# A retention and mixture-of-experts kernel: operand preparation cut into steps, loads moved, second-weight sums from GpSimd to VectorE, last block stored in halves

## Chip, cores and metric

One core of a Trainium2 chip runs the whole kernel. The metric is the device time of one execution in microseconds: the median of several runs. The profile is one more execution, recorded by the hardware profiler. The engines are TensorE (PE in the profile; its weight loads are PEld), VectorE (DVE), ScalarE (ACT), GpSimd (POOL) and SyncE (SP), which here only issues transfers.

## The reference

The kernel computes retention (attention with a decaying state, batch 4, 8 heads, 768 positions, head size 64) and feeds its output to a mixture of 8 experts whose gate is normalised by 8 Sinkhorn rounds.

```python
for t in range(S):                      # retention
    state = gamma * state + outer(k[:, :, t], v[:, :, t])
    y[:, :, t] = scale * q[:, :, t] @ state
x = y as (3072, 512)

P = exp(x @ w_gate - max)               # gate
for _ in range(8):
    P /= P.sum(1, keepdims=True) + 1e-09
    P /= P.sum(0, keepdims=True) + 1e-09
    P *= N / E
for e in range(8):                      # experts
    h = maximum(x @ w1[e], 0.0)         # (3072,512) @ (512,1024)
    out += P[:, e:e + 1] * (h @ w2[e])  # (3072,1024) @ (1024,512)
```

## The kernel before

**Numbers in two parts.** Every operand of a large product is held as a rounded high part (fp32r) and a low remainder: `hi_act` (line 77) rounds on ScalarE, `lo` (line 80) subtracts the high part from the full value, on VectorE or GpSimd. A product is then three matmuls: high*high, low*high, high*low.

**Seven products for eight.** Both expert layers use a Strassen-like scheme: the 2x2 block products are made with seven products, called M1 to M7, on sums and differences of blocks. The operands of M1, M2, M3 and M7 (for x) or M1, M2, M4 and M7 (for w1) are loaded; the other three are made by four additions or subtractions.

**Opening stage: attention by blocks.** There are 24 blocks of 128 positions (6 chunks of 4 batches). Step `tau` of a loop written out by hand does, in this order: scale the keys of block tau (`decay_k`, L348, GpSimd), issue loads of block tau+3, split q and k of block tau+2 (`split_qk`: ScalarE rounds kh and QH, GpSimd makes kl, VectorE makes QL), scores of block tau+1 (L367 on PE, mask `ta` L370 on VectorE), gate logits of block tau-1, output of block tau (`attend`, L395 and L400 on PE, `RX` L404 on VectorE, stored to DRAM as `xd`), state update (`hold`, L379 on PE). Engines run their instructions in program order, and SP too. After steps 2 to 10 the remaining 13 blocks ride along in the rows of the next stage (`chunk(g, m)`), one block a row.

**First layer: 96 rows.** A unit (`UnitA`) is 256 columns of w1 (a job) on one third of x. A row n runs seven products in the order of `ROW`: (unit n: M6), (unit n+1: M1), (n: M3), (n: M7), (n+1: M2), (n+1: M5), (n: M4); m = 0 to 6 is the place in a row. Four PSUM banks are shared: the next product on a bank waits until VectorE (L213, L218, L225) or ScalarE (L207, L209, L211, L219, L226, L229) has read the one before. `sums` and `last_sum` make the sums that the second layer needs; all seven results are stored in DRAM as `hd`. In a row with attention, `chunk` adds one part at each m: m = 0 `decay_k` and `attend`, 1 logits, 2 scores, 3 `split_qk`, 4 `hold`, 5 loads.

**Preparing operands.** `w1_load(n)` brings job n's block into one of two halves of RW; `w1_tasks` makes its operand WA: four additions on GpSimd (L158) and two roundings on ScalarE in one task, then two remainders on VectorE as two tasks. A row takes one task at m = 0, 1 and 5. `x_load` brings a third of x from `xd` in eight transfers; `x_tasks` makes its operand in 22 tasks (two halves k of 4 subtractions and 7 roundings with remainder), shared between VectorE and GpSimd by a list. x of the first third (X0) is prepared in steps 9 and 10, that of the second (X1) from row 15 on VectorE alone, that of the third (X0 again) from row 33. Sinkhorn's 23 pieces (`sink`) come one after each of rows 26 to 47, the last after row 60.

**Second layer: 24 units of 28 parts.** `UnitB` is one expert on one third of x (experts in reverse). A part is a quarter (q) of a product: six matmuls. `b_part(s)` runs part s, evaluates a finished product (`post`, `emit`: L627, L629, L631 on VectorE, stored from SP for the first expert and by an accumulating GpSimd transfer, L636, for the others), issues loads of later h parts and converts part s+5 (`h_conv`: ScalarE rounds, VectorE makes the remainder). Beside it the next expert's w2 is prepared in two blocks f = 0, 1: `w2_load`, four subtractions on GpSimd (L719), then three roundings and three remainders; these tasks stand in a queue `bq`, one taken at q = 0, 2 and 3 of each product.

Of the kernel before, what the change touches and what calls it, by code (L numbers as in the profile page):

```python
# [28 lines left out]
NJ = E * QE  # L29
# [18 lines left out]
def kernel(  # L48
# [60 lines left out]
    def x_load(t, r):  # L109
        for i, c, d in ((M1, 0, 0), (M7, 1, 0), (M3, 1, 1), (M2, 0, 1)):  # L110
            for k in range(2):
                sp.dma_start(rd(t[:, XP[i], 1, k * 512:(k + 1) * 512]).rearrange("p (b s) -> p b s", s=C),
                             xd[2 * r + c][:, :, 2 * d + k, :])

    def x_tasks(t, engs):
        q = []
        sc = {M7: 0, M5: 1, M6: 2, M4: 3}
        e = [engs[k % len(engs)] for k in range(22)]
        for k in range(2):
            def w(i, a=1, k=k):  # L120
                return t[:, XP[i], a, k * 512:(k + 1) * 512]

            def src(i, w=w):
                return XSC[:, sc[i], :] if i in sc else rd(w(i))

            def tt(o, a, b, src=src):
                eng = e.pop()
                q.append(lambda: eng.tensor_tensor(XSC[:, sc[o], :], a, b, ALU.subtract))

            def one(i, w=w, src=src):  # L130
                eng = e.pop()

                def f():
                    hi_act(w(i, 0), src(i))
                    lo(eng, w(i, 1), src(i), w(i, 0))
                q.append(f)

            b12 = rd(w(M7))
            tt(M5, b12, src(M1))
            tt(M6, src(M3), src(M5))  # L140
            tt(M7, src(M3), b12)
            tt(M4, src(M2), src(M6))
            for i in (M1, M5, M2, M6, M7, M3, M4):
                one(i)
        return q
# [8 lines left out]
    def w1_tasks(n, eng_add, eng_lo):  # L154
        a, x = WA[n % 3], w1_raw(n)

        def tt(o, p, q, op):
            eng_add.tensor_tensor(x[:, WP[o]], x[:, WP[p]], x[:, WP[q]], op)  # L158

        def adds():  # L160
            tt(M5, M7, M4, ALU.add)
            tt(M6, M5, M1, ALU.subtract)
            tt(M3, M2, M6, ALU.subtract)
            tt(M7, M1, M7, ALU.subtract)
            hi_act(a[:, 0:3, 0, :], x[:, 0:3, :])
            hi_act(a[:, 3:7, 0, :], x[:, 3:7, :])

        def rest(s):
            lo(eng_lo, a[:, s, 1, :], x[:, s, :], a[:, s, 0, :])

        return [adds, lambda: rest(slice(0, 3)), lambda: rest(slice(3, 7))]
# [85 lines left out]
    with tc.manual_schedule():  # L257
# [6 lines left out]
        if True:  # L264
# [184 lines left out]
            for tau in range(2, LAST):  # L449
                if tau == 2:  # L450
                    loads(4)
# [4 lines left out]
                if tau < LAST - 2:  # L456
                    loads(tau + 3)
                else:
                    loads(tau + 3, (1, 3) if tau == LAST - 2 else (1,))
                if tau < LAST - 1:  # L460
                    split_qk(tau + 2)
                scores(tau + 1)
                logits(tau - 1)
                attend(tau)
                for t in late.get(tau, [tau]):
                    hold(t)
                if tau >= LAST - 2:
                    loads(tau + 3, (0, 2))
                if tau == 4:
                    w1_load(0)  # L470
                    w1_load(1)
                    todo += w1_tasks(0, pool, dve) + w1_tasks(1, pool, dve)
                if tau == 2 * B - 1:
                    x_load(X0, 0)
                if tau == 2 * B:
                    todo += x_tasks(X0, [dve, pool, dve])
                if tau in (6, 7):
                    run(todo, 3)
                if tau > 2 * B:
                    run(todo, 8)  # L480
# [119 lines left out]
        class UnitB:  # L600
# [37 lines left out]
            def post(self, i):  # L638
# [19 lines left out]
                elif i == M7:  # L658
                    self.emit(1, 1, ps, s5)
                elif i == M4:  # L660
                    self.emit(1, 0, ps, None)
# [55 lines left out]
        def w2_tasks(e, f):  # L717
            def tt(o, a, b):
                return lambda: pool.tensor_tensor(w2x[:, VP[o]], w2x[:, VP[a]], w2x[:, VP[b]], ALU.subtract)  # L719
# [9 lines left out]
            def two(a, b):  # L729
                return [lambda: hi(a, b), lambda: rest(a, b)]  # L730

            q, t, none = [tt(*x) for x in w2t], two(0, 3), [lambda: None]
            return ([lambda: w2_load(e, f)] + none * 6 + q[:2] + t[:1] + q[2:3] + t[1:] + q[3:] + none * 2
                    + two(3, 5) + two(5, 7))

        bq = []
# [3 lines left out]
        def b_part(s):  # L740
# [11 lines left out]
            e, g = divmod(u.n, NPAIR)  # L752
            if q != 1:
                run(bq, 1)
            if g == 0 and i == M6 and q == 0 and e + 1 < E:
                bq.extend(w2_tasks(e + 1, 0) + w2_tasks(e + 1, 1))
# [4 lines left out]
        w1_load(2)  # L761
# [4 lines left out]
        loaded = 3  # L766
        PS2 = None
        carry = None
        for n, u in enumerate(UA):
# [15 lines left out]
            if n == NJ + 1:  # L785
                xq = x_tasks(X0, [dve, pool])
# [9 lines left out]
            for m, (k, i) in enumerate(ROW):  # L796
# [8 lines left out]
                if m in (0, 1, 5):  # L805
# [3 lines left out]
                if m in (1, 6) or n >= NJ:  # L809
# [14 lines left out]
            if 26 <= n < 25 + len(sink):  # L824
                sink[n - 26]()
            if n == 60:
# [4 lines left out]
        for s in range(6, 9):  # L831
            h_conv(s)
        for s in range(4, len(parts)):
# [52 lines left out]
```

## Time and profile before

| | |
|---|---|
| median of 3 runs | 2089.88 us (2088.89 to 2090.1) |
| the profiled execution | 2088.59 us; span 2086.8 us |
| busy: PE, PEld | 1995.7 us, 1644.4 us |
| busy: VectorE, ScalarE, GpSimd | 1581.3, 1043.7, 532.3 us |
| transfers | 505.19 MB, mean 242 GB/s |

A row of a timeline gives start, duration, engine, line, operation, out<-in, shape and count; brackets hold the idle time of the engine before it and what ended it. A row of the view of waits gives the waiting instruction, what it waited for, the total in us, the number of times and the longest. A window row gives the stretch, its length, the busy time of each engine with its number of instructions, the granted share of the TensorE clock, the share of the transfer engines and GB/s. A row of the chain gives start, duration and what it was. Several equal instructions in succession are merged.

### The profile page before, as it was taken

The numbers are of one execution on the slowest core, as the hardware profiler recorded it, in microseconds if no ns is written. First come the engines' busy times: TensorE is split into PE (matmuls) and PEld (weight loads), VectorE is DVE, ScalarE is ACT, GpSimd is POOL, SyncE is SP. The second block draws the span as 40 slices with busy tenths as digits, with TensorE's granted clock in tenths as the row PEclk, the third lists the DMA queues.
The fourth block names the chain that finished last, engine by engine and source line by source line (L and its number), as shares of the span: only waits on it lengthen the run. The fifth ranks groups of instructions, "written<-read, shape, count | busy, mean of one in ns | idle before, by whom it ended". The sixth has DMA issues, their size and how long they took to land.

```text
span 2086.8 us, 28805 instructions
## 1 busy us (share of the span) xinstructions
PE 1995.7 (96%) x9273; PEld 1644.4 (79%) x9273; DVE 1581.3 (76%) x2024; ACT 1043.7 (50%) x1674; POOL 532.3 (26%) x498
## 2 busy tenths in 40 slices
PE   7689999999899999999999999999999999999997
PEld 7578887887688888888886887887878787787886
DVE  6778878987787666666667787878788787968765
ACT  3334445654444444444445555555555555555553
POOL 4655633341421221221132101112021111202001
PEclk9789999999999999999999999999999999999999
DMA  7547668777476666666667989999999999999996
GB/s 257 163 135 244 216 225 276 250 246 247 160 234 212 227 219 218 215 232 217 220 236 262 305 269 269 269 278 268 260 285 255 277 271 274 263 288 258 263 264 157
DMA packets 253337, 505.19 MB, mean 242 GB/s; under 512 B 27840, under 2 KB 40448, under 8 KB 251136
## 3 DMA queue, kind: packets, MB, share of 16 engines
q1 hardware_dynamic: 241088, 459.30, 66.0%
q0 software_dynamic: 12096, 44.05, 11.5%
q8 instruction: 72, 1.18, 0.2%
q14 instruction: 81, 0.66, 0.1%
HBM read 270.36 MB, written 232.88 MB: 241 GB/s over the span
## 4 chain that ended last, share of the span: by engine, by line
PE 72%; DVE 9%; DMA 7%; issue 5%; POOL 1%; ACT 1%; SPq 0%; DVEq 0%; POOLq 0%; ACTq 0%
PE psA L190 38%; PE psA L618 19%; PE psB L618 13%; DMA WA<-hd 5%; DVE WA L80 4%; POOL RW L158 1%; DMA rn<-kn 1%; DVE QL L80 1%; DVE X L80 1%; DMA hd<-OT 1%; DVE XSC L629 1%; PE psa L367 0%; DMA RW<-w 0%; DVE OT L240 0%; DVE OT L234 0%
## 5 line engine op out<-in xcount | busy, mean ns | idle before, releaser
L190 PE MATMUL psA<-X,WA 128*128 128x512 f32 x4032 | 942.8, 394 | 18.2 <-DVE OT L213 8.1
L190 PEld LDWEIGHTS psA<-X,WA 128*128 128x128 f32 x4032 | 757.1, 189 | 183.6 <-ACT OT L229 12.3
L618 PE MATMUL psA<-WA,X 128*128 128x512 f32 x2296 | 539.0, 391 | 18.9 <-DVE WA L80 18.7
L77 ACT ACTIVATE WA<-WA 128x512 fp32r<-128x512 f32 x668 | 402.9, 629 | 270.3 <-PE psB L618 117.5
L618 PEld LDWEIGHTS psA<-WA,X 128*128 128x128 f32 x2296 | 428.6, 188 | 118.5 <-DVE WA L80 29.3
L80 DVE TENSOR_TENSOR WA<-WA,WA 128x512 fp32r<-128x512 f32 x487 | 363.7, 791 | 108.4 <-ACT WA L77 99.6
L618 PE MATMUL psB<-WA,X 128*128 128x512 f32 x1728 | 406.0, 391 | 7.3 <-ACT WA L77 3.9
L158 POOL TENSOR_TENSOR RW<-RW 128x256 f32<-128x256 f32 x256 | 243.0, 959 | 573.7 <-DMA RW<-w 348.3
L618 PEld LDWEIGHTS psB<-WA,X 128*128 128x128 f32 x1728 | 323.7, 188 | 79.6 <-DVE WA L80 8.0
L219 ACT ACTIVATE OT<-OT 128x512 f32<-128x512 f32 x96 | 60.7, 632 | 267.6 <-DVE OT L218 267.6
L80 DVE TENSOR_TENSOR WA<-RW,WA 128x768 fp32r<-128x768 f32 (+1 forms) x128 | 155.8, 1217 | 49.0 <-ACT WA L77 47.2
L80 DVE TENSOR_TENSOR WA<-WA 128x512 fp32r<-128x512 f32 x181 | 139.5, 798 | 38.2 <-ACT WA L77 34.0
L636 POOL DMA_DIRECT2D out<-XSC x57 | 49.6, 870 | 465.0 <-DVE XSC L631 248.2
L213 DVE TENSOR_TENSOR OT<-psA,OT 128x512 f32<-128x512 f32 x96 | 66.1, 689 | 99.2 <-PE psA L190 99.1
L77 ACT ACTIVATE WA<-RW 128x768 fp32r<-128x768 f32 (+1 forms) x128 | 115.1, 947 | 34.9 <-POOL RW L158 24.9
L719 POOL TENSOR_TENSOR RW<-RW 128x512 f32<-128x512 f32 x56 | 86.5, 1582 | 89.1 <-DMA RW<-w 57.4
L226 ACT ACTIVATE OT<-OT 128x512 f32<-128x512 f32 x96 | 60.7, 632 | 93.6 <-DVE OT L225 93.6
L225 DVE TENSOR_TENSOR OT<-psA,OT 128x512 f32<-128x512 f32 x96 | 66.2, 690 | 51.3 <-ACT OT L219 45.3
L236 DVE TENSOR_TENSOR OT<-OT 128x512 f32<-128x512 f32 x96 | 91.6, 954 | 3.3
L646 ACT ACTIVATE OT<-psA 128x512 f32<-128x512 f32 x96 | 57.4, 598 | 72.0 <-PE psA L618 68.0
L229 ACT ACTIVATE OT<-psA 128x512 f32<-128x512 f32 x96 | 57.4, 597 | 69.6 <-PE psA L190 40.8
L240 DVE TENSOR_TENSOR OT<-OT 128x512 f32<-128x512 f32 x96 | 75.3, 785 | 20.6 <-ACT OT L229 17.5
(166 smaller groups left out, 1517.1 us busy)
## 6 DMA issues: line engine op xcount, KB each, us to landing
hd<-OT SPq DMA_DIRECT2D x672, 256.0 KB, 2.8
WA<-hd SPq DMA_DIRECT2D x668, 256.0 KB, 6.0
RW<-w SPq DMA_DIRECT2D x64, 512.0 KB, 4.5
out<-XSC POOLq DMA_DIRECT2D x57, 512.0 KB, 8.2
RW<-w SPq DMA_DIRECT2D x16, 1024.0 KB, 8.4
out<-OT POOLq DMA_DIRECT2D x27, 512.0 KB, 8.1
OT<-pd SPq DMA_DIRECT2D x23, 512.0 KB, 7.4
xd<-RX SPq DMA_DIRECT2D x24, 256.0 KB, 5.1
```

The source lines that it names most:

```text
L77: act.activation(o, i, AF.Copy)
L80: eng.tensor_tensor(o, full, rd(h), ALU.subtract)
L158: eng_add.tensor_tensor(x[:, WP[o]], x[:, WP[p]], x[:, WP[q]], op)
L190: pe.matmul(ps, w[:, a, k * P:(k + 1) * P], x[:, b, k * 512:(k + 1) * 512], start=i in PRE and k == 0 and m == 0, stop=k == 1 and m == 2, ...
L213: dve.tensor_tensor(c12, ps, u2, ALU.add)
L219: act.activation(o, o, AF.Relu)
L225: dve.tensor_tensor(o, ps, s1, ALU.add)
L226: act.activation(o, o, AF.Relu)
L236: dve.tensor_tensor(t["S2"], t["S1"], t["A11"], ALU.subtract)
L240: dve.tensor_tensor(self.new("S4"), self.t["A12"], self.t["S2"], ALU.subtract)
L618: pe.matmul(ps[d] if isinstance(ps, tuple) else ps[:, d, :], w[:, a, q * 256 + d * P:q * 256 + d * P + P], h[b], start=i in PRE and q == 0 ...
L719: return lambda: pool.tensor_tensor(w2x[:, VP[o]], w2x[:, VP[a]], w2x[:, VP[b]], ALU.subtract)
```

## The change

- `x_load` can load one of its two source chunks alone. For the first third of x, chunk 0 is issued after step 5 and chunk 1 after step 8, instead of both after step 7.
- `x_tasks` becomes 11 steps for each half: step n does one subtraction (n < 4, always VectorE) or one remainder, and, for n < 7, the rounding that a later step (three to five on) needs. Of the remainders GpSimd has two in seven where the list is `[dve, dve, pool]`. In steps 9 and 10 of attention two of them stand in each of five places instead of eight at the end.
- `w1_tasks` has four tasks: additions, rounding, remainder, remainder. Jobs 0 and 1 are spread over steps 5 to 8. `w1_load(2)` moves from the start of the rows to step 7, `w1_load(3)` from the end of row 0 to step 8. In rows the tasks stand at m = 0, 3, 5 and 6; at m = 3 the task is ahead of `chunk(g, 3)`, that is of `split_qk`.
- x tasks of the third third run at all m but 2.
- Sinkhorn's pieces start after row 39, the last after row 62.
- w2's subtractions run on VectorE, one at each q of M1; rounding and remainders stand in M5 and the first quarter of M4, block f = 0 in the expert's first row of products, f = 1 in the second. `w2_load` of block 1 is issued in M4 of the first row, that of the next expert's block 0 in the third row; for expert 1 ahead of the second layer's loop.
- The last output block is not accumulated by GpSimd: its old value is loaded, VectorE adds it, and SP stores it in two halves.

```diff
-    def x_load(t, r):
-        for i, c, d in ((M1, 0, 0), (M7, 1, 0), (M3, 1, 1), (M2, 0, 1)):
-            for k in range(2):
+    def x_load(t, r, which=(0, 1)):
+        for i, c, d in ((M1, 0, 0), (M2, 0, 1), (M7, 1, 0), (M3, 1, 1)):
+            for k in range(2) if c in which else ():
...
+            def step(n, w=w, src=src):
+                b12 = rd(w(M7))
+                hi = [M1, M2, M5, M6, M7, M3, M4][n] if n < 7 else None
+                if n < 4:
+                    o, a, b = [(M5, b12, src(M1)), (M6, src(M3), src(M5)), (M7, src(M3), b12), (M4, src(M2), src(M6))][n]
+                    dve.tensor_tensor(XSC[:, sc[o], :], a, b, ALU.subtract)
+                else:
+                    i = [M1, M5, M2, M6, M7, M3, M4][n - 4]
+                    lo(engs[n % len(engs)], w(i, 1), src(i), w(i, 0))
+                if hi is not None:
+                    hi_act(w(hi, 0), src(hi))
+
+            q += [lambda n=n, step=step: step(n) for n in range(11)]
...
+        def rounded():
             hi_act(a[:, 0:3, 0, :], x[:, 0:3, :])
             hi_act(a[:, 3:7, 0, :], x[:, 3:7, :])
...
-        return [adds, lambda: rest(slice(0, 3)), lambda: rest(slice(3, 7))]
+        return [adds, rounded, lambda: rest(slice(0, 3)), lambda: rest(slice(3, 7))]
...
+                some = (lambda: run(todo, 2)) if tau > 2 * B else lambda: None
...
-                    todo += w1_tasks(0, pool, dve) + w1_tasks(1, pool, dve)
-                if tau == 2 * B - 1:
-                    x_load(X0, 0)
-                if tau == 2 * B:
-                    todo += x_tasks(X0, [dve, pool, dve])
-                if tau in (6, 7):
-                    run(todo, 3)
-                if tau > 2 * B:
-                    run(todo, 8)
+                    wt = w1_tasks(0, pool, dve), w1_tasks(1, pool, dve)
+                if 5 <= tau <= 8:
+                    k = tau - 5
+                    for f in (wt[0][:1], wt[0][1:2] + wt[1][:1], wt[0][2:] + wt[1][1:2], wt[1][2:])[k]:
+                        f()
+                if tau == 5:
+                    x_load(X0, 0, (0,))
+                if tau == 7:
+                    w1_load(2)
+                if tau == 8:
+                    w1_load(3)
+                    x_load(X0, 0, (1,))
+                    todo += x_tasks(X0, [dve, dve, pool])
...
+                elif i == M4 and self.n < len(UB) - 1:
+                    self.emit(1, 0, ps, None)
                 elif i == M4:
-                    self.emit(1, 0, ps, None)
+                    o = out[2 * self.r + 1, 0].rearrange("p (d t) -> p d t", d=2)
+                    sp.dma_start(TB[0], o)
+                    for d in range(2):
+                        y, t = YS[0][:, d], [t for x, t in ps if x.start <= d < x.stop][0]
+                        dve.tensor_tensor(y, t[:, d % t.shape[1]], PB[1 + self.n % 2][:, 1, :], ALU.mult)
+                        dve.tensor_tensor(y, y, TB[0][:, d], ALU.add)
+                        sp.dma_start(o[:, d], y)
...
-                return lambda: pool.tensor_tensor(w2x[:, VP[o]], w2x[:, VP[a]], w2x[:, VP[b]], ALU.subtract)
+                return lambda: dve.tensor_tensor(w2x[:, VP[o]], w2x[:, VP[a]], w2x[:, VP[b]], ALU.subtract)
...
+            return {(f, M1, x): [t[x]] for x in range(4)} | {
+                (f, M5, 0): [h[0], r[0]], (f, M5, 1): [h[1]], (f, M5, 2): [r[1]], (f, M5, 3): [h[2]],
+                (f, M4, 0): [r[2]]}
...
+                if (g, i, q) == (0, M4, 1):
+                    w2_load(e + 1, 1)
+                if (g, i, q) == (2, M6, 0) and e + 2 < E:
+                    w2_load(e + 2, 0)
...
-                xq = x_tasks(X0, [dve, pool])
+                xq = x_tasks(X0, [dve, dve, pool])
...
-                if m in (0, 1, 5):
+                if m in (0, 3, 5, 6):
                     run(wq, 1)
                 if n < NROW:
                     chunk(LAST + n, m)
-                if m in (1, 6) or n >= NJ:
+                if m in (1, 6) or n >= NJ and m != 2:
                     run(xq, 1)
...
-            if 26 <= n < 25 + len(sink):
-                sink[n - 26]()
-            if n == 60:
+            if 39 <= n < 38 + len(sink):
+                sink[n - 39]()
+            if n == 62:
                 sink[-1]()
...
+        w2_load(1, 0)
         for s in range(4, len(parts)):
             b_part(s)
```

More of the change, by code (lines that the diff above doesn't have):

```diff
@@ L117, in x_tasks @@
         sc = {M7: 0, M5: 1, M6: 2, M4: 3}
-        e = [engs[k % len(engs)] for k in range(22)]
         for k in range(2):
@@ L124, in src @@
                 return XSC[:, sc[i], :] if i in sc else rd(w(i))
[L126 to L144, printed above, removed]
+            def step(n, w=w, src=src):
[10 more added lines that the diff above has]
+            q += [lambda n=n, step=step: step(n) for n in range(11)]
         return q
@@ L459 @@
                     loads(tau + 3, (1, 3) if tau == LAST - 2 else (1,))
+                some()
                 if tau < LAST - 1:
                     split_qk(tau + 2)
+                some()
                 scores(tau + 1)
+                some()
                 logits(tau - 1)
                 attend(tau)
+                some()
                 for t in late.get(tau, [tau]):
                     hold(t)
+                some()
                 if tau >= LAST - 2:
@@ L727, in rest @@
                 lo(dve, t[:, :, 1], w2x[:, a:b], t[:, :, 0])
[L729 to L736, printed above, removed]
+            t = [tt(*x) for x in w2t]
+            h = [lambda a=a, b=b: hi(a, b) for a, b in ((0, 3), (3, 5), (5, 7))]
+            r = [lambda a=a, b=b: rest(a, b) for a, b in ((0, 3), (3, 5), (5, 7))]
+            return {(f, M1, x): [t[x]] for x in range(4)} | {
+                (f, M5, 0): [h[0], r[0]], (f, M5, 1): [h[1]], (f, M5, 2): [r[1]], (f, M5, 3): [h[2]],
+                (f, M4, 0): [r[2]]}
+        w2p = {}
         nload = [NHL + 4]
@@ L751, in b_part @@
                 h_conv(s + 5)
[L752 to L756, printed above, removed]
+            e, g = divmod(u.n - (i in PRE), NPAIR)
+            if u.n >= (i in PRE) and e + 1 < E:
+                if (g, i, q) == (0, M6, 0):
+                    w2p.clear()
+                    w2p.update(w2_tasks(e + 1, 0) | w2_tasks(e + 1, 1))
+                for f in w2p.get((g, i, q), ()):
+                    f()
+                if (g, i, q) == (0, M4, 1):
+                    w2_load(e + 1, 1)
+                if (g, i, q) == (2, M6, 0) and e + 2 < E:
+                    w2_load(e + 2, 0)
         wq, xq = [], []
         NROW = NCHUNK - LAST + 1
-        w1_load(2)
         loaded = conv = 2
@@ L765 @@
             UA[0].post(i)
-        loaded = 3
+        loaded = 4
         PS2 = None
```

## The prediction

> **What bounds the kernel now.** First the page's busy table, slices and chain.
>
> ```profile
> PE 1995.7 (96%) x9273; PEld 1644.4 (79%) x9273; DVE 1581.3 (76%) x2024; ACT 1043.7 (50%) x1674; POOL 532.3 (26%) x498
> PE   7689999999899999999999999999999999999997
> PE 72%; DVE 9%; DMA 7%; issue 5%; POOL 1%; ACT 1%; SPq 0%; DVEq 0%; POOLq 0%; ACTq 0%
> ```
>
> TensorE (PE) is busy nearly everywhere and makes 72% of the chain, so the change can only win its idle places: the first three slices and small stalls later. The view of waits, for PE, names these:
>
> ```profile
> PE psA L618 <- DVE WA L80: 18.7, 22, 1.5
> PE psA L190 <- DVE OT L213: 8.1, 3, 4.2
> PE psa L395 <- DVE ta L370: 6.4, 1, 6.4
> PE psa L379 <- POOL rn L348: 6.3, 1, 6.3
> PE psA L190 <- ACT OT L229: 6.3, 11, 1.2
> ```
>
> PE waits for conversions in the second stage (L618), twice in the rows where the third x is prepared (L213), once each in attention and in row 1 (L395, L379), and a little in each of the rows that carry attention (L229). I price these five places and the end of the program.
>
> **1. Attention up to row 0 (40 to 112 us): loads and x preparation moved.**
>
> ```profile
> 65.62 6.21 SPq L112 DMA_DIRECT2D X<-xd  x8
> 78.17 0.63 ACT L77 ACTIVATE WA<-OT 128x512 fp32r<-128x512 f32 x1 [9.20 <-DMA OT<-kT]
> 40.00:112.00 72.00, 50.47 (x339) 44.42 (x338) 55.05 (x65) 22.61 (x37) 45.45 (x35) 0.79 0.50 164
> 102.25 0.69 DVE L128 TENSOR_TENSOR XSC<-X,XSC 128x512 f32<-128x512 f32 x1
> X<-xd SPq DMA_DIRECT2D x24, 256.0 KB, 5.4
> ```
>
> In the window rows the third to seventh numbers are busy PE, PEld, DVE, ACT and POOL. Eight x transfers hold SP's queue for 6.21 us ahead of block 11's k; ACT waits 9.20 us for it, VectorE behind ACT, and PE 6.4 us behind VectorE's ta (the third row of waits). The change issues four at step 5 (half, 3.1 us) ahead of block 9's loads, which have a whole step to land, and four at step 8. The wait comes back elsewhere: at step 7 SP waits with w1_load(2) until VectorE has finished job 0's remainders (behind it: block 11's loads), at step 8 with w1_load(3) for job 1's, and the second half of x follows. VectorE's first x step at step 9 reads M7 of that half, so VectorE stands about 5.4 us for it, with block 11's split queued behind. I keep 6.5 us of wait there. VectorE is idle 72.0 - 55.05 = 17 us of this stretch now; of the other 10.5 us I let three stay, as the steps no longer wait for ACT's rounding and POOL's part is smaller. VectorE takes 18 of the 22 x operations instead of 15: 3 x 0.69 = 2.1 us. Sum -10.5 + 3 + 2.1 = -5.4, say **-6** (ACT no longer waits for POOL's sums before its split); bounds -10 (idle time gone) and +3 (the second half lands one more 5.4 us late, less what filling saves). w1's sums on POOL one step earlier stand before decay_k(6), whose products PE has before a split it waits for anyway: 0, and 1.5 us if that split came sooner. x steps of rows 15 to 25 stay on VectorE with rounding one step ahead of them: 0, since PE has no wait for X there to lose.
>
> **2. Row 1's missing weights.**
>
> ```profile
> 130.72 1.42 SPq L152 DMA_DIRECT2D RW<-w  x2
> 138.29 3.60 POOL L158 TENSOR_TENSOR RW<-RW 128x256 f32<-128x256 f32 x4 [14.17 <-DMA RW<-w]
> 127.02 1.05 PE L395 MATMUL psa<-rq,st 128*128 128x128 f32 x8
> 151.34 1.05 PE L395 MATMUL psa<-rq,st 128*128 128x128 f32 x8
> ```
>
> Job 3's block is issued only at 130.72; POOL waits 14.17 us with decay_k queued behind, and PE 6.3 us for decay_k (L348 in the view of waits). From row 1's attention to row 2's it takes 24.3 us; a steady row, below, 15.5. The change loads job 3 in step 8, so **-8.8**. Bounds -9.4 (if the row then runs at PE's own 15.0: 15.5 less PE's 0.5 of waiting, below) and, if job 4 is late in its place, -2. SP's loads of later jobs wait for the remainder in product 6 instead of 5, 1.4 us later; they are issued two rows ahead of their use, so 0.
>
> **3. Rounding moved to product 3 of a row: a cost.** The steady row with attention:
>
> ```profile
> 242.78 0.69 DVE L225 TENSOR_TENSOR OT<-psA,OT 128x512 f32<-128x512 f32 x1
> 246.26 1.79 ACT L77 ACTIVATE WA<-RW 128x768 fp32r<-128x768 f32 x2
> 254.07 0.63 ACT L219 ACTIVATE OT<-OT 128x512 f32<-128x512 f32 x1 [5.53 <-DVE OT L218]
> 255.77 2.51 DVE L80 TENSOR_TENSOR QL<-rq,QH 64x512 fp32r<-64x512 f32 x2 [1.74 <-ACT QH L77]
> 258.31 0.69 DVE L225 TENSOR_TENSOR OT<-psA,OT 128x512 f32<-128x512 f32 x1
> 261.47 0.73 PE L190 MATMUL psA<-X,WA 128*128 128x512 f32 x2 [0.49 <-ACT OT L229]
> ```
>
> L225 to L225 is 15.53 us: VectorE works from L225 to L218 (M7's sum with s5, which L219 waits for), waits 1.74 us while ACT does L219 and the split's rounding, does QL, and reaches L225; from there ACT's L229 frees the bank PE waits for. ACT's 1.79 us of weight rounding now stands in ACT's idle 5.53 us. `rounded` at m == 3 is emitted after L219 and before split_qk, so ACT runs it inside VectorE's wait: 1.74 + 1.79 = 3.53 us, a row of 17.3. Rows 0 to 10 have a split: 11 x 1.79 = **+19.7**. Bounds: 0 if a cover exists that I don't see, and +25 with the clock: PE's gap grows from 0.5 to about 2.3 us.
>
> ```profile
> 50.40:53.80 3.40, 1.31 (x9) 0.92 (x8) 2.07 (x2) 2.62 (x4) 2.57 (x2) 1.00 1.00 372
> 53.80:57.20 3.40, 2.66 (x13) 2.66 (x13) 3.32 (x7) 0.00 (x0) 3.24 (x5) 0.51 0.09 30
> ```
>
> After 3.4 us with 1.31 us of PE work the granted clock (third number from the end) was 0.51. A gap of 2.3 us leaves 1.1 us of work in such a stretch, if the stretch holds it whole. Half clock for 3.4 us costs PE 1.7 us, in half of 11 rows +9; VectorE's chain sets the row and hides part of it, so I take +5.5. The Trainium skill (TensorE: Matmul & The Clock Gate, section Why this matters for your kernels) asks only that no gap exceed about 3 us; by that rule the +5.5 is excluded and the sum stays as below, while the row with two gaps of a us each, at half clock after it, shows that shorter ones can do it.
>
> **4. Rows 32 to 36 (third x) and Sinkhorn.**
>
> ```profile
> 527.29 1.06 ACT L77 ACTIVATE WA<-RW 128x1024 fp32r<-128x1024 f32 x1 [4.38 <-POOL RW L158]
> 531.12 11.81 PE L190 MATMUL psA<-X,WA 128*128 128x512 f32 x42 [4.15 <-DVE OT L213]
> 500.00:560.00 60.00, 50.88 (x204) 40.04 (x203) 48.44 (x68) 27.50 (x48) 29.92 (x23) 0.91 0.64 201
> 600.00:900.00 300.00, 299.11 (x1324) 247.24 (x1323) 200.31 (x285) 139.75 (x223) 55.93 (x65) 1.00 0.65 221
> ```
>
> ACT stands 4.38 us behind POOL's w1 sums; the x operands and then VectorE's L213 stand behind ACT; PE loses 8.1 us idle (L213 in the view of waits) and, at a mean clock of 0.91, 0.09 x 60 = 5.4. Three products between sums and rounding cover POOL's 4 us, and Sinkhorn is gone from these rows. VectorE is still fuller than a row (five x operations of 0.69 on some 7 us), so 3 us stay: **-10.5**, bounds -13.5 and -4. Sinkhorn in rows 39 to 62 costs 0: VectorE is busy 200 of 300 us there; were it full, PE would lose in those rows what it saves in these. P is then ready two rows later, some thirty before its first use.
>
> **5. The second stage: sums from POOL to VectorE.**
>
> ```profile
> 1290.20 4.36 DVE L80 TENSOR_TENSOR WA<-WA,WA 128x512 fp32r<-128x512 f32 x2
> 1291.18 2.81 POOL L719 TENSOR_TENSOR RW<-RW 128x512 f32<-128x512 f32 x2
> 1355.89 10.88 PE psA L618 x48
> 1409.07 4.38 DVE WA L80 x2
> 1528.05 4.38 DVE WA L80 x2
> 1350.00:1388.00 38.00, 38.00 (x169) 31.45 (x169) 26.40 (x38) 19.85 (x33) 3.45 (x4) 1.00 0.94 267
> RW<-w SPq DMA_DIRECT2D x16, 1024.0 KB, 8.4
> ```
>
> Two conversions take 4.36 us instead of 1.3 while POOL sums (2.81): VectorE gets almost nowhere beside POOL, and PE then waits (18.7 us in 22 places, the first row of waits). An expert takes 1528.05 - 1409.07 = 118.98 us; its 504 products at 10.88 for 48 need 114.24: 4.74 us lost, in six experts 28.4. On VectorE four sums are 4 x 0.69 = 2.8 us a row, remainders 1.74 + 2 x 1.22 = 4.2: with the clean row's 26.4 it is 33.4 of 38.1 us, no overload. The second block is issued in M4 and lands 8.4 us later, about 1 us after VectorE wants it, with conversions queued behind; these run five parts (6.8 us) ahead, so 0.6 us an expert stays: **-25**; bounds -28 and 0. Issuing the first block before expert 0 puts 4 us of transfer ahead of its h loads: **+1**, bounds 0 and +4.
>
> **6. The last block.**
>
> ```profile
> 2075.47 1.37 DVE L627 TENSOR_TENSOR XSC<-psA,OT 128x512 f32<-128x512 f32 x2 [3.29 <-PE psA L618]
> 2077.14 0.86 POOL L636 DMA_DIRECT2D out<-XSC  x1 [3.80 <-DVE XSC L627]
> out<-XSC POOLq DMA_DIRECT2D x57, 512.0 KB, 8.2
> hd<-OT SPq DMA_DIRECT2D x672, 256.0 KB, 2.8
> ```
>
> Now the store starts at 2077.14 and lands 8.2 us later. Then VectorE does 4 x 0.69 from 2075.47 and SP stores at 2078.2, landing 2.8 later at 2081.0 instead of 2085.3: **-4.3**. The load of the old block waits for nothing recent; YS[0]'s earlier store lands about when it is needed. Bounds -5 and -1.
>
> **Sum.** -6 - 8.8 + 19.7 - 10.5 - 25 + 1 - 4.3 = -33.9 us on the profiled execution's 2088.59: 2054.7. The three runs' median is 1.3 above it: **2056 us**.
>
> **Rivals.** *Rounding is hidden* (rows keep 15.5 us): 2056 - 20 = 2036; ACT's 5.53 us of idle time speaks for it, but ACT runs in order, against it. *Start and clock bad*: part 1 at +3 and half clock in rows, 2056 + 9 + 5.5 = 2070. *The sums only change engines*, and VectorE still loses PE its 4.7 us: 2056 + 25 = 2081; 33.4 of 38.1 us speaks against it. *On the other side*: the second block lands so late that VectorE stands on its first sum with all conversions behind it. To end slower than now by 4 us, the experts would have to lose 28.4 + 13 = 41 us, 6.9 each, beyond a lead of some 4.8 us (6.8 less about 2 for a conversion itself); the block would have to land about 20 us after its issue, against 8.4: over 2094. PE's 72% of the chain and a transfer share of 0.94 leave that unlikely, not excluded.
>
> **How the numbers follow.** Forecast 0.60 (its own range 2046 to 2066), hidden rounding 0.10, bad start 0.14, sums only moved 0.08, between 2086 and 2094 0.03, other side 0.05. Range 2037 to 2074 leaves some two in ten out. Changes within 0.2% (4 us) can't be told from none: faster 0.91, same 0.04, slower 0.05.
>
> **What would show it.** Step 3: L225 to L225 at 17.3 us, VectorE's wait before QL at 3.5. Step 2: no wait of L379 for L348. Step 4: no wait above 2 us for L213. Step 5: no POOL sums, experts 114.5 to 115 apart. Step 6: some 6 us from PE's end to the last landing. Experts still at 119, or PE waiting for conversions after the sums, would make it wrong; so would rows at 15.5.

## The result: the change is slower, 2102.9 us

| | median | range | ratio to before, 95% interval |
|---|---|---|---|
| before | 2089.88 us | 2086.03 to 2091.91 | |
| after | 2102.91 us | 2100.74 to 2112.02 | 1.0074, 1.0059 to 1.0089 |

The forecast was 2056 us. The profiled execution of after took 2102.91 us with a span of 2101.1 (before 2086.8), so the two traces differ by 14.3 us and can be compared directly.

The page after: busy engines, two rows of slices, the chain.

```profile
PE 2016.9 (96%) x9273; PEld 1669.0 (79%) x9273; DVE 1558.5 (74%) x2092; ACT 1037.9 (49%) x1674; POOL 443.9 (21%) x431
PE   8688898999999999999999999999999999999998
PEclk9788889999999999999999999999999999999999
PE 85%; DVE 7%; issue 3%; ACT 2%; DMA 2%; SPq 0%; POOL 0%; DVEq 0%; ACTq 0%
```

The same 9273 matmuls are busy 21 us longer. That points at the clock, and in the slices of 52.5 us the granted clock is low in the second (the opening, as before) and, which is new, in the third to sixth, 105 to 315 us: the rows with attention. The view of waits for PE says the same. Line numbers shift: L221, L225, L186 and L624 after are L225, L229, L190 and L618 before.

```profile
PE psA L186 <- ACT OT L225: 25.1, 16, 2.5
PE psA L186 <- DVE WA L80: 14.6, 16, 2.0
PE psa L391 <- DVE ta L366: 14.3, 1, 14.3
PE psB L624 <- ACT WA L77: 3.2, 2, 3.0
```

The wait for the bank (L225 on ACT) was 6.3 us in 11 places and is 25.1 in 16. In the opening the wait for `ta` has grown from 6.4 to 14.3 us. The wait for a remainder of the first weights (WA, line 80) is new. The 18.7 us that the second layer lost to conversions are gone, and so is the wait of row 1 for `decay_k`.

The work between two starts of L221 is one row. Where the 14.3 us come from, by these starts (differences taken before rounding):

| stretch | before | after | difference |
|---|---|---|---|
| up to the start of the rows | 113.7 | 111.3 | -2.4 |
| rows 0 to 10 (with a split) | 174.4 | 222.7 | +48.3 |
| rows 11 to 32 | 218.1 | 222.3 | +4.1 |
| rows 33 to 36 (third x) | 53.2 | 49.8 | -3.4 |
| rows 37 to 94 | 555.6 | 558.3 | +2.7 |
| from there to the end of the span | 971.7 | 936.7 | -35.0 |

So the second layer, the end and row 1's wait brought their gains, and rows 0 to 10 took more than all of it. One of them in the timeline of after; L221 starts at 212.14 and at 234.61, 22.5 us apart instead of 15.5:

```profile
212.14 0.69 DVE L221 TENSOR_TENSOR OT<-psA,OT 128x512 f32<-128x512 f32 x1
...
214.65 0.60 ACT L225 ACTIVATE OT<-psA 128x512 f32<-128x512 f32 x1 [0.66 <-issue]
215.11 1.03 POOL L344 TENSOR_TENSOR rn<-rn,gk 128x512 f32<-128x512 f32 x1
215.30 0.51 PE L186 MATMUL psA<-X,WA 128*128 128x512 f32 x1 [1.58 <-ACT OT L225]
215.35 3.60 DVE L80 TENSOR_TENSOR WA<-RW,WA 128x768 fp32r<-128x768 f32 x2
216.11 1.75 POOL L399 TENSOR_TENSOR st<-st,dec 128x512 f32<-128x512 f32 x1
217.02 2.50 PE L186 MATMUL psA<-X,WA 128*128 128x512 f32 x5 [1.22 <-DVE WA L80]
...
223.59 0.41 PE L363 MATMUL psa<-QH,kh 128*128 128x256 f32 x1
...
228.69 0.63 ACT L215 ACTIVATE OT<-OT 128x512 f32<-128x512 f32 x1 [8.47 <-DVE OT L214]
229.22 1.78 ACT L77 ACTIVATE WA<-RW 128x768 fp32r<-128x768 f32 x2
...
232.07 2.51 DVE L80 TENSOR_TENSOR QL<-rq,QH 64x512 fp32r<-64x512 f32 x2 [3.42 <-ACT QH L77]
234.61 0.69 DVE L221 TENSOR_TENSOR OT<-psA,OT 128x512 f32<-128x512 f32 x1
```

Read it from the bottom. VectorE waits 3.42 us for QH because ACT rounds the weights (1.78 us) first: this is what step 3 forecast (3.5). From there the row's L221, ACT's L225 and PE's bank are late: 1.58 us of idle PE. Then comes what the prediction did not have. The remainder of the slices that the next product M1 reads (128x768) used to be made at m = 1 of a row; at m = 5 it stands behind the state update, right in front of that M1, and PE stops a second time, 1.22 us, after a single matmul.

That remainder has also become slower. The rows below are the group of this one operation in rows 2 to 8, first before, then after: times it ran, total us, mean ns, idle us ahead of it. At m = 1 it takes 0.95 us; at m = 5 it runs beside GpSimd's scaling of keys and state (L344, L399) and takes 1.62. In row 9 of after GpSimd has nothing to scale: the remainder takes 0.96 us and PE waits 0.57 us for it (third row), and though the first gap is 1.58 us again, the clock of the row stays at 1.00 (fourth row). This is one row; no run takes the collision alone away.

```profile
L80 DVE TENSOR_TENSOR WA<-RW,WA 128x768 fp32r<-128x768 f32 x7 | 6.6, 948 | 0.0
L80 DVE TENSOR_TENSOR WA<-RW,WA 128x768 fp32r<-128x768 f32 x7 | 11.3, 1616 | 0.1
303.72 1.41 PE L186 MATMUL psA<-X,WA 128*128 128x512 f32 x5 [0.57 <-DVE WA L80]
299.50:316.90 17.40, 15.26 (x99) 12.78 (x100) 12.26 (x16) 6.78 (x11) 5.82 (x6) 1.00 0.63 197
```

And then PE itself is slow: a score matmul takes 0.41 us here, 0.28 in e4 below. In three windows, the third number from the end is the granted clock; the last one is of the kernel before:

```profile
213.40:223.40 10.00, 7.20 (x26) 5.68 (x23) 6.78 (x8) 2.27 (x5) 4.46 (x4) 0.65 0.96 288
147.20:299.50 152.30, 132.75 (x660) 112.26 (x660) 96.93 (x113) 47.49 (x77) 60.04 (x50) 0.81 0.53 168
148.50:258.30 109.80, 107.33 (x667) 92.29 (x667) 95.31 (x112) 46.85 (x77) 62.01 (x50) 1.00 0.71 233
```

The second row holds rows 2 to 8: mean clock 0.81 over 152.3 us, where the kernel before had 1.00 over 109.8 (third row).

### The profile page after: what moved, and what is told of

It reads as the page before. It is cut to its first block, busy times and chain, and to the rows that moved or that the text cites. A ratio compares the mean times of both kernels' runs of the same rounds, so it can differ in the third digit from the quotient of the medians.

```text
span 2101.1 us, 28837 instructions
## 1 busy us (share of the span) xinstructions
PE 2016.9 (96%) x9273; PEld 1669.0 (79%) x9273; DVE 1558.5 (74%) x2092; ACT 1037.9 (49%) x1674; POOL 443.9 (21%) x431
## 3 DMA queue, kind: packets, MB, share of 16 engines
q0 software_dynamic: 11952, 43.52, 10.7%
## 4 chain that ended last, share of the span: by engine, by line
PE 85%; DVE 7%; issue 3%; ACT 2%; DMA 2%; SPq 0%; POOL 0%; DVEq 0%; ACTq 0%
PE psA L186 39%; PE psA L624 25%; PE psB L624 19%; DVE WA L80 2%; DVE QL L80 1%; PE psa L363 1%; ACT WA L77 1%; DMA hd<-OT 1%; PE psl L405 1%; DVE OT L230 1%; DVE X L80 0%; DVE st L381 0%; DVE OT L221 0%; DMA rk<-kT 0%; DVE XSC L131 0%
## 5 line engine op out<-in xcount | busy, mean ns | idle before, releaser
L186 PE MATMUL psA<-X,WA 128*128 128x512 f32 x4032 | 962.1, 398 | 42.9 <-ACT OT L225 25.1
L186 PEld LDWEIGHTS psA<-X,WA 128*128 128x128 f32 x4032 | 765.0, 192 | 215.8 <-ACT OT L225 30.8
L624 PE MATMUL psA<-WA,X 128*128 128x512 f32 x2296 | 531.4, 389 | 0.2 <-DVE XSC L635 0.2
L624 PEld LDWEIGHTS psA<-WA,X 128*128 128x128 f32 x2296 | 430.9, 188 | 90.1 <-issue 0.6
L624 PE MATMUL psB<-WA,X 128*128 128x512 f32 x1728 | 404.2, 390 | 4.5 <-ACT WA L77 3.2
L80 DVE TENSOR_TENSOR WA<-WA,WA 128x512 fp32r<-128x512 f32 x487 | 313.7, 685 | 99.4 <-ACT WA L77 88.6
L624 PEld LDWEIGHTS psB<-WA,X 128*128 128x128 f32 x1728 | 324.6, 188 | 74.1 <-ACT WA L77 4.1
L152 POOL TENSOR_TENSOR RW<-RW 128x256 f32<-128x256 f32 x256 | 257.8, 1017 | 564.9 <-DMA RW<-w 472.3
L209 DVE TENSOR_TENSOR OT<-psA,OT 128x512 f32<-128x512 f32 x96 | 66.2, 690 | 172.0 <-PE psA L186 171.7
L80 DVE TENSOR_TENSOR WA<-RW,WA 128x768 fp32r<-128x768 f32 (+1 forms) x128 | 170.1, 1367 | 0.1
L80 DVE TENSOR_TENSOR WA<-WA 128x512 fp32r<-128x512 f32 x181 | 122.0, 698 | 36.1 <-ACT WA L77 32.3
L203 ACT ACTIVATE OT<-psA 128x512 f32<-128x512 f32 x96 | 57.5, 599 | 107.7 <-PE psA L186 107.7
L221 DVE TENSOR_TENSOR OT<-psA,OT 128x512 f32<-128x512 f32 x96 | 66.3, 691 | 54.0 <-ACT OT L215 45.5
L232 DVE TENSOR_TENSOR OT<-OT 128x512 f32<-128x512 f32 x96 | 91.3, 951 | 3.3
L652 ACT ACTIVATE OT<-psA 128x512 f32<-128x512 f32 x96 | 57.4, 598 | 73.3 <-PE psA L624 69.4
L207 ACT ACTIVATE OT<-psA 128x512 f32<-128x512 f32 x96 | 57.4, 598 | 56.2 <-PE psA L186 56.2
L236 DVE TENSOR_TENSOR OT<-OT 128x512 f32<-128x512 f32 x96 | 69.5, 724 | 19.1 <-ACT OT L225 19.0
```

What stands on the lines that cost most here:

```text
L80: eng.tensor_tensor(o, full, rd(h), ALU.subtract)
L186: pe.matmul(ps, w[:, a, k * P:(k + 1) * P], x[:, b, k * 512:(k + 1) * 512], start=i in PRE and k == 0 and m == 0, stop=k == 1 and m == 2, ...
L203: act.activation(s1, ps, AF.Copy)
L209: dve.tensor_tensor(c12, ps, u2, ALU.add)
L221: dve.tensor_tensor(o, ps, s1, ALU.add)
L232: dve.tensor_tensor(t["S2"], t["S1"], t["A11"], ALU.subtract)
```

## The experiments

Theory 1: the two moved tasks on the first weights (rounding ahead of the split; remainders ahead of M1) lengthen the rows, each by its own wait, and the two waits together halve the clock. Rival: the rows are slow for another reason, such as the new opening loads. Runs of one group shared a chip, with the kernel before beside them: its median was 2086.6 us beside e1 to e4, 2088.2 beside e5, e6, e7 and e10, and 2088.7 beside e8, e9, e11 and e12. Across groups the ratios are compared; a difference of two ratios is uncertain by some 0.002, or 4 us, and smaller effects are read from the traces.

| run | median us | ratio to before, 95% | rows 2 to 8, us each | clock there |
|---|---|---|---|---|
| after | 2102.91 | 1.0074 (1.0059 to 1.0089) | 21.8 | 0.81 |
| e1, w1 tasks back | 2033.78 | 0.9745 (0.9730 to 0.9759) | 15.5 | 1.00 |
| e2, only remainders moved | 2051.98 | 0.9833 (0.9819 to 0.9848) | 16.7 | 0.99 |
| e3, only rounding's place | 2059.88 | 0.9874 (0.9857 to 0.9890) | 17.9 | 0.95 |
| e4, after with filler matmuls | 2076.40 | 0.9947 (0.9932 to 0.9962) | 18.6 | 0.97 |
| e7, after, rounding behind the split | 2058.65 | 0.9861 (0.9846 to 0.9877) | 16.9 | 0.97 |
| e5, e1 with new order, sums on GpSimd | 2036.33 | 0.9752 (0.9735 to 0.9768) | | |
| e11, e1 with old order, sums on VectorE | 2037.09 | 0.9750 (0.9736 to 0.9765) | | |
| e12, e1 with old order, sums on GpSimd | 2064.75 | 0.9886 (0.9870 to 0.9903) | | |
| e6, e1 with job 3's load late | 2039.52 | 0.9769 (0.9755 to 0.9784) | | |
| e10, e1 with x ahead of jobs 2 and 3 | 2029.04 | 0.9721 (0.9707 to 0.9736) | | |
| e8, e1 with last block by GpSimd | 2039.41 | 0.9764 (0.9750 to 0.9779) | | |
| e9, e1 with Sinkhorn early | 2037.35 | 0.9753 (0.9738 to 0.9767) | | |

### Both moved tasks back (e1)

```diff
-                if m in (0, 3, 5, 6):
-                    run(wq, 1)
+                if m in (0, 1, 5):
+                    run(wq, 2 if m == 0 else 1)
```

> The changed kernel with the tasks on the first weights called where they were before the change: two in the first chunk product (sums and rounding), one in the second, one in the sixth; all else as changed. Theory 1 (the new places of the w1 tasks lengthen the loop of rows 2 to 10, and the gaps they open halve the TensorE clock): these rows return from about 21.5 us to about 15.5, the waits of L186 on DVE WA L80 and of ta L186 on ACT OT L225 fall away, and rows 0 to 10 take 162.8 - 15 = about 150 us instead of 208; rows 33 to 35 may give back 3 to 5 us. Time about 2045 to 2055 us. Rival 2 (the rows are slow because of the new order of the opening loads): rows stay at 21 to 22 us and the time stays within 2095 to 2105.

2033.78 us, 69 us under after, 53 under before and 11 under the range expected. Every row from 1 to 8 takes 15.5 us. In the view of waits, PE in 140 to 310 us has one row left; the window of rows 2 to 8 follows:

```profile
PE psA L186 <- ACT OT L225: 5.8, 10, 0.8
```

```profile
137.80:246.50 108.70, 105.07 (x660) 90.45 (x659) 95.09 (x112) 46.67 (x77) 61.95 (x50) 1.00 0.71 235
```

The rival falls: the opening is unchanged in this kernel. The cost of the two moved tasks in the two traces, 69.2 us, is 55.6 in rows 0 to 10 and 4.1 in rows 11 to 32, then 6.0 in rows 33 to 36 (43.8 us here), 1.4 in the later rows, and 2.0 in the opening, which this edit does not touch: in the eleven kernels with this same opening the first L221 lies between 108.2 and 112.2 us.

### Each task alone (e2, e3, e7)

e2:

```diff
-                if m in (0, 3, 5, 6):
-                    run(wq, 1)
+                if m in (0, 5, 6):
+                    run(wq, 2 if m == 0 else 1)
```

> The changed kernel with sums and rounding of the first weights back in the first chunk product, but the two remainder tasks left where the change put them (sixth and seventh). It tells the two moved tasks apart. Theory 1a (the rounding in front of the split is the first cause; the remainders cost only their extra wait of under a microsecond a row): rows 2 to 10 at 16.0 to 16.5 us at a full clock, time 2050 to 2060. Theory 1b (the remainder task that now stands in front of the next row's first matmul, with the wait of 1.2 us behind it, is the main cost): rows at 18.5 us or more, time 2075 to 2090. Rival 2: rows at 21 or more, time about 2100.

e3, on top of e1 (its second rounding writes the same values again):

```diff
+                    if m == 0:
+                        again = wq[1] if len(wq) == 4 else None
...
+                if m == 3 and n < NROW - 3 and again is not None:
+                    again()
```

> The first experiment's kernel, with the rounding of the first weights run a second time in the fourth chunk product, ahead of the split, in the rows before the last three of the weights; the remainders stand where they were before the change. It measures the place of the rounding alone. The prediction's sum (1.8 us a row from one VectorE operation ahead of the split): rows at 17.3 us, time 20 us over the first experiment, about 2070. With its bound for a halved clock: 17.8, about 2075. If the place of the rounding alone explains everything: rows at 21 or more, about 2100. If the operation is hidden: rows as in the first experiment.

e7, on top of after:

```diff
-                if m in (0, 3, 5, 6):
+                if m in (0, 5, 6):
                     run(wq, 1)
                 if n < NROW:
                     chunk(LAST + n, m)
+                if m == 3:
+                    run(wq, 1)
```

> The changed kernel with one edit: the task of the fourth chunk product (the rounding of the first weights) is called behind the chunk's part, that is behind the split of q and k, instead of ahead of it. The remainders stand as changed. If the place ahead of the split is what made the rounding cost: rows as in the second experiment, 16.4 to 16.5 us, time 2048 to 2056. Rival (any rounding in that part of the row costs, since the matmuls' bank L225 reads on ScalarE is then late): rows at 18 us or more, time over 2070.

e2 is theory 1a: rows of 16.4 and 16.5, one of 18.0. Its timeline has the second wait and not the first:

```profile
189.83 0.49 PE L186 MATMUL psA<-X,WA 128*128 128x512 f32 x1
189.86 3.60 DVE L80 TENSOR_TENSOR WA<-RW,WA 128x768 fp32r<-128x768 f32 x2
191.54 1.42 PE L186 MATMUL psA<-X,WA 128*128 128x512 f32 x5 [1.22 <-DVE WA L80]
...
200.53 2.51 DVE L80 TENSOR_TENSOR QL<-rq,QH 64x512 fp32r<-64x512 f32 x2 [1.74 <-DMA hd<-OT]
```

e3 has the first and not the second, with rows of 17.2 and two of 19.7:

```profile
145.72 1.90 PE L186 MATMUL psA<-X,WA 128*128 128x512 f32 x6 [3.00 <-ACT OT L225]
...
199.85 1.65 PE L186 MATMUL psA<-X,WA 128*128 128x512 f32 x6 [2.16 <-ACT OT L225]
...
211.37 2.50 DVE L80 TENSOR_TENSOR QL<-rq,QH 64x512 fp32r<-64x512 f32 x2 [3.42 <-ACT QH L77]
```

17.2 is the prediction's 17.3. The rounding that e3 repeats runs on ScalarE; its expectation wrongly calls it a VectorE operation. The time is 26 us over e1 where 20 were expected; the two rows of 19.7, at a lowered clock, make up 5 of the 6 us between. e7 shows that the place ahead of the split makes the cost, not the rounding: behind it, rows take e2's 16.4 (two of 18.0). Its time is 3 us over what was expected; against e2, rows 0 to 10 take 3.2 us more and rows 33 to 36 take 48.1 us against 45.1. From the start of row 0 to the end of row 10, e1 takes 167.1 us, e2 8.5 more, e3 23.4 more. Their sum is 31.9; after takes 55.6 more. The two tasks together cost 24 us that neither costs alone.

### The clock by itself (e4)

```diff
+                if m == 0 and n < NROW - 3:
+                    for _ in range(12):
+                        pe.matmul(pslx[:, 256:512], X0[:, 0, 0, 0:P], X0[:, 0, 0, 0:256], start=True, stop=True, **kw)
```

> The changed kernel with 12 matmuls more in each row before the last three of the weights, behind attend, whose results are not used (they fill the gap in which TensorE waits). It tells the clock from the waits. If the halved clock costs 3 to 4 us a row: clock 1.00 in rows 2 to 10, rows at 17.5 to 18.5 us, time about 2065 to 2075. If the clock follows the waits without a price of its own, rows stay at 21 to 22 us or grow by the added matmuls' 1.3 us, time 2100 to 2115.

The tile of the logits is widened to give these matmuls a place to write. After with more work for PE is 26.5 us faster, 2076.40 us, 1.4 over the range expected for a clock with a price of its own. The row in its timeline:

```profile
200.84 1.70 PE L832 MATMUL psl<-X 128*128 128x256 f32 x12
201.86 0.60 ACT L225 ACTIVATE OT<-psA 128x512 f32<-128x512 f32 x1 [0.68 <-issue]
202.51 0.50 PE L186 MATMUL psA<-X,WA 128*128 128x512 f32 x1
...
204.25 1.41 PE L186 MATMUL psA<-X,WA 128*128 128x512 f32 x5 [1.24 <-DVE WA L80]
...
207.79 0.28 PE L364 MATMUL psa<-QH,kh 128*128 128x256 f32 x1
```

The chain that sets the waits is unchanged (ACT's L225 starts 2.52 us behind L221, 2.51 in after; the remainder still costs PE 1.24 us), but the score matmuls run at 0.28 instead of 0.41 us. Most rows take 18.1 us, which is 15.5 + 0.9 (e2's typical row) + 1.7 (e3's): the two waits add up, and the rest of the 21.2 to 22.5 us is the clock, 3 to 4 us a row. Over rows 0 to 10 it is 28.7 us more than e1, near the 31.9 of the two tasks alone. Theory 1 is shown in its three parts: two waits and the clock. That GpSimd has a part in the second wait, as row 9 above suggests, was not in it.

### The second weights: engine or order (e5, e11, e12)

e5 on top of e1; e11 and e12 put back the old queue of tasks, on VectorE and GpSimd:

```diff
-                return lambda: dve.tensor_tensor(w2x[:, VP[o]], w2x[:, VP[a]], w2x[:, VP[b]], ALU.subtract)
+                return lambda: pool.tensor_tensor(w2x[:, VP[o]], w2x[:, VP[a]], w2x[:, VP[b]], ALU.subtract)
```

> The first experiment's kernel, with the four subtractions of the second weights back on GpSimd (L727), at their new places, M1, while the conversions stay in M5 and M4. It tells the engine from the order. Theory 1 (GpSimd's sums hold up VectorE's conversions beside them): the sums take 2.8 us for two, each holds VectorE up by about as much as the sum itself lasts, once in a quarter of M1; experts at 116 to 119 us instead of about 114, time 10 to 28 us over the first experiment's 2033.8. Rival (the gain came from the order, with conversions well apart from the sums): within 4 us of 2033.8.

> The first experiment's kernel with the second weights' tasks in their old order and places (one queue, a task in three of four parts, transfers as before), but the four subtractions on VectorE. With the fifth experiment (new order, GpSimd) and the next run it makes a table of engine by order. If the engine was the cause: within 4 us of the first experiment's 2033.8, the conversions at 0.69 us, and the second stage 937 to 940 us from the last row to the end. If the order was the cause: PE waits for conversions again, the second stage 950 to 965 us, time 2045 to 2062.

> The first experiment's kernel with the second weights' tasks in their old order and on GpSimd, as before the change: the whole fifth step of the prediction undone. By the prediction's 25 less 1: time 2033.8 + 24 = 2057.8. By the second stage of the two traces (971.7 to 936.7 us, less 6 for the end of the program): + 29 = 2063. Either way it has to be at least 20 us over the first experiment, or the step's gain came from elsewhere.

Undone whole (e12), the step costs 29.4 us by ratio (0.0141 of 2088), and 29.6 between the traces from the last row to the end (966.3 against 936.6). Half undone, either way, it costs nothing that these intervals can tell, and next to nothing in the traces: the same stretch takes 937.6 us in e5 and 936.6 in e11. Waits of PE in the second layer of e12, then the sums and the conversions beside them in e5's timeline:

```profile
PE psA L624 <- DVE WA L80: 18.7, 22, 1.5
```

```profile
1288.64 6.06 POOL L734 TENSOR_TENSOR RW<-RW 128x512 f32<-128x512 f32 x4 [2.73 <-DMA RW<-w]
...
1290.22 7.44 DVE L80 TENSOR_TENSOR WA<-WA,WA 128x512 fp32r<-128x512 f32 x7 [3.05 <-ACT WA L77]
```

In e5 seven conversions take 7.44 us instead of 4.8 (7 x 0.69): GpSimd's sums still slow VectorE. From 1200 to 2000 us a conversion takes 773 ns on average there, 801 in e12 and 685 in e11 and after, where VectorE does the sums, which is 38 us of lost VectorE time in e5 and 48 in e12. Most of the collision is still there in e5, but PE no longer waits for it. So the loss needed both, the collision and the old order. That VectorE had no slack at the old places, because the weights' own roundings and remainders stood there, is the likely reason; no run tests it.

### The opening (e6, e10)

```diff
 e6:
                 if tau == 8:
-                    w1_load(3)
...
-        loaded = 4
+        loaded = 3
 e10:
                 if tau == 7:
-                    w1_load(2)
+                    x_load(X0, 0, (1,))
                 if tau == 8:
+                    w1_load(2)
                     w1_load(3)
-                    x_load(X0, 0, (1,))
```

> The first experiment's kernel, with job 3's first weights loaded after row 0 again instead of in step 8 of attention. It measures the second step of the prediction by itself. The prediction's step: row 1 takes 23 to 24 us instead of 15.5, time 2033.8 + 8.8 = 2042.6, with PE waiting 6 us for decay_k. Rival (the early load costs the opening about as much as it saves in row 1, since it stands ahead of the second half of x on SP's queue): row 0 comes up to 5 us earlier and the time is 2036 to 2039.

> The first experiment's kernel with the second half of x loaded in step 7 and both blocks of first weights (jobs 2 and 3) in step 8, instead of job 2 in step 7 and job 3 ahead of x in step 8. VectorE's wait of 4.6 us for the second half of x in step 9, and most of PE's 13.4 us for ta behind it, should go if that transfer is the cause: row 0 4 to 8 us earlier, time 2026 to 2030. Rival (block 11's loads, then behind the x transfers on SP's queue, are late in its place): row 0 as before or later, 2034 to 2040.

In e6 row 1 takes 23.0 us again, 7.5 more, with the old wait (first row below, of e6), but the rows' first L221 comes at 106.4 us, 2 to 6 earlier than in the eleven kernels, since the weights no longer stand ahead of x on SP's queue: VectorE's waits for x in the opening fall from 6.0 us in e1 to 3.5. Net it is 5 us by ratio and 3.4 between the traces, between the two expectations. In e10 the wait for `ta` falls from 13.4 us in e1 to 8.8 (second row, of e10), and the kernel is 5 us faster by ratio, 4.1 between the traces: 2029.04 us, the fastest of all, 2.8% under before. The transfer was a cause of the wait, and not the only one.

```profile
PE psa L375 <- POOL rn L344: 6.3, 1, 6.3
```

```profile
PE psa L391 <- DVE ta L366: 8.8, 1, 8.8
```

### The end and Sinkhorn (e8, e9)

e8 stores the last block by `self.emit(1, 0, ps, None)` as before; e9:

```diff
-            if 39 <= n < 38 + len(sink):
-                sink[n - 39]()
-            if n == 62:
+            if 26 <= n < 25 + len(sink):
+                sink[n - 26]()
+            if n == 60:
```

> The first experiment's kernel with the last output block accumulated by GpSimd's transfer again. The prediction's sixth step: + 4.3 us, 2038. The traces' tails (9.95 us from PE's end to the span's end before, 3.84 after): + 6, 2040. Rival (the store was hidden): 2034.

> The first experiment's kernel with Sinkhorn's pieces after rows 26 to 48 again instead of 39 to 61. Rows 32 to 36 took 53.2 us before and 43.8 in the first experiment; this tells how much of the 9.4 is Sinkhorn's. If the pieces (softmax sums on VectorE and ScalarE between rows) were what filled VectorE there: these rows at 48 to 53 us, time 2037 to 2043. If the steps of x and the three products between sums and rounding did it: 44 to 45 us, time 2033 to 2035.

e8 costs 4.0 us by ratio, 4.4 between the traces from the last row to the end. The 9.95 and 3.84 us of its expectation run from VectorE's last operation; from PE's last matmul to the end it is 10.7 us before and 6.0 after, which fits. In e9 rows 33 to 36 (its expectation calls them 32 to 36) take 48.1 us instead of 43.8 (PE's wait for L209 there is 4.9 us, below, against 2.3), but 1.2 us come back later, where Sinkhorn stood in e1. The net 3.1 is 1.7 by ratio, which alone could not be told from zero.

```profile
PE psA L186 <- DVE OT L209: 4.9, 2, 3.1
```

## Why the prediction was wrong

**Step 3 is the one that failed.** It priced the moved rounding at +19.7 us with +25 as its bound; the moved tasks cost 69. Three things were missing. The step looked only at rounding: that the remainders, moved from m = 1 and 5 to m = 5 and 6, now stand in front of the M1 that reads them was visible in the code, and their rows (1.87 and 0.95 us on VectorE) in the trace before, but step 3 gave them no price: 18 us by the medians (e2), 8.5 of it in rows 0 to 10. The remainder that M1 needs also meets the collision with GpSimd that the prediction described in its own step 5: it takes 1.62 us in its new place instead of 0.95, and row 9 of after, without the collision, suggests that more than half of PE's second wait comes from this. The rounding itself had the right size, 17.2 against 17.3 us a row, and 23.4 us in rows 0 to 10 with two half-clock rows (e3), inside the bound of +25. And the clock was priced at 5.5 us, as a bound, for one gap of 2.3 us in half of the rows. With two gaps, 1.58 and 1.22 us with one matmul between, it halved for a part of each of rows 2 to 8: 24 us more. The row that showed half clock after a 3.4 us stretch with 1.31 us of work was in the prediction (its two gaps are 1.05 and 1.78 us, the second running past the stretch); the new row has about 0.5 us of work in 3.3. The Trainium skill, page TensorE: Matmul & The Clock Gate, section Why this matters for your kernels, asks that no idle gap between bursts of matmuls exceed about 3 us. Each gap here is under 1.6 us, so trace and rule differ, and the measurement decides.

**The forecast was an addition of single prices.** With 69 in the place of 19.7 its own sum would have given 2105, 2 us from the measurement. That the rest of the sum fits so well is luck: steps 1, 2 and 4 brought less than forecast, step 5 brought 5 us more, and the misses cancel.

**The other steps.** Step 1: -6 forecast; row 0's attention is 4.8 us earlier in the trace, the first L221 2.4 (1.5 to 5.6 in the eleven kernels with this opening). Its rest of 6.5 us of waiting for x was 6.0 on VectorE, 4.6 of it in one wait. Step 2: the wait went as forecast, but the early load takes some of it back in the opening, so it was worth 3 to 5 us instead of 8.8 (e6). Step 2's bound of -9.4 should read -9.3 by its own rows (24.3 - 15.0). Step 4: -10.5 forecast, -3.4 in after, because the same rounding and remainders stand in these rows; without them -9.4 (e1), 4.3 of it Sinkhorn's (e9), which the prediction did not separate. Step 5: -24 net forecast, -29.4 measured (e12): not even the 0.6 us an expert that it kept was left. Its reading of the collision was right and its remedy half of the story: moving the sums to VectorE and moving them in time each do it alone. Of after, the groups of conversions and sums from 1200 to 2000 us and the window that answers to the one shown of before:

```profile
L80 DVE TENSOR_TENSOR WA<-WA,WA 128x512 fp32r<-128x512 f32 x433 | 279.0, 685 | 84.5 <-ACT WA L77 76.9 <-DMA WA<-hd 6.3
L734 DVE TENSOR_TENSOR RW<-RW 128x512 f32<-128x512 f32 x56 | 38.3, 684 | 0.0
```

```profile
1350.00:1388.00 38.00, 38.00 (x169) 31.46 (x168) 32.00 (x45) 22.97 (x36) 3.43 (x4) 1.00 0.95 290
```

The conversions take 685 ns each where they took 801 before (and again 801 in e12), and 32.0 of 38 us on VectorE agree with the forecast 33.4 of 38.1. Step 6: -4.3 forecast, 4.0 to 4.4 measured (e8). The end of after:

```profile
2094.51 0.69 DVE L674 TENSOR_TENSOR OT<-psA,OT 128x512 f32<-128x512 f32 x1 [3.28 <-PE psA L624]
2095.24 0.69 DVE L675 TENSOR_TENSOR OT<-OT 128x512 f32<-128x512 f32 x1
2095.85 0.68 DVE L674 TENSOR_TENSOR OT<-psA,OT 128x512 f32<-128x512 f32 x1
2095.96 1.67 SPq L676 DMA_DIRECT2D out<-OT  x2
2096.56 0.69 DVE L675 TENSOR_TENSOR OT<-OT 128x512 f32<-128x512 f32 x1
```

**The rivals.** None was the one that came. The one on the other side was put in the second layer, where nothing went wrong; the rows, where a cost was already known, had no rival that doubled it.

## What to carry to other kernels

When a task moves in a row that repeats, write down for each engine what it now stands in front of and who reads its result next: here the rounding was no longer than before, and the new neighbours made the two tasks cost 69 us. Look also at what runs on the other engines at the new place: beside GpSimd the remainder took 1.62 us instead of 0.95. Two small waits on the engine that bounds a stage can cost more than their sum: where they lie close together, price the clock with them, and look at the clock of the windows before believing the waits. When a gain comes from an edit with two halves, undo each half alone before naming the cause; here either half of the second-weight edit was enough.

## What the hardware showed

Two idle places of 1.58 and 1.22 us on TensorE with a 0.5 us matmul between were followed by a halved clock in each of rows 2 to 8 (0.65 over the 10 us around them, 0.81 over these rows). With 1.58 and 0.57 us, in row 9, the clock stayed at 1.00. In rows 1 to 9 of e3 the clock fell in the row with a single gap of 3.00 us and in one of five rows with a single gap of 2.16 us (0.95 over rows 2 to 8). With a single gap of 1.22 us it fell in one of rows 1 to 8 in e2 (0.99) and in two in e7 (0.97). Twelve matmuls of 128x256 whose results nobody reads, 1.7 us, put into the first of the two gaps brought the clock from 0.81 to 0.97 in rows 2 to 8 and made the kernel 26.5 us faster.

A VectorE subtraction of 128x768 took 0.95 us alone and 1.62 beside GpSimd's multiplications of 128x512.
